# Sparse attention and a mixture-of-experts layer on one core: the gate value spread by a transfer, first weights in pieces of two blocks, v of two pairs ahead of q, a new order with more filler matmuls

## The chip, the cores and the metric

The kernel runs on one core of one Trainium2 chip. The metric is device time in microseconds (us) of the whole program, lower is better. Engines are named as in the profile: PE (matmul), PEld (weight loads of PE), DVE, ACT, POOL and SP; POOL and SP also issue DMA transfers.

## The reference

```python
# attention: q, k, v are [4 batches, 8 heads, 768 rows, 64]
block, window = (32, 16)
k_sum = k.reshape(B, H, nb, block, D).max(axis=3)
v_sum = v.reshape(B, H, nb, block, D).mean(axis=3)
scores_l = scale * np.matmul(q, k.transpose(0, 1, 3, 2))        # kept where |i - j| < 16
scores_s = scale * np.einsum('bhsd,bhnd->bhsn', q, k_sum) + np.log(block)
a = softmax(concatenate([masked scores_l, scores_s]))
attn = np.matmul(a, np.concatenate([v, v_sum], axis=2))
# mixture of experts: x is attn as [4, 768, 512]; 8 experts, F = 1024
pooled = x.mean(axis=1)
logits = pooled @ w_gate
e_idx = np.argmax(logits, axis=1)                   # one expert for each batch
gate_w = softmax(logits)[e_idx]
out[b] = gate_w[b] * (np.maximum(x[b] @ w1[e_idx[b]], 0) @ w2[e_idx[b]])
```

The expert of a batch is known only when the attention of that batch is done, so its weights (w1 and w2, 2 MB each in float32) can only be fetched then.

## The kernel before

There are four batches, and in each the 8 heads go as 4 pairs (pr 0 to 3). The work of a pair is: transpose k and q (T; in batches 1 to 3 one step for both, which takes two PSUM banks), copy them out of PSUM (own, qo), maxima over blocks of 32 (kmx, rest), scores on PE (S, two halves u), exp on ACT, mask on DVE (batches 1 to 3), weights times v on PE (O), division by the sum on DVE (norm), transpose back on PE (X), copy to xT on ACT (xo), whose running sum gives the pooled x. Vs sums v over blocks on PE, once for two pairs in batch 0 and once for four pairs in the others; DVE spreads the sums over the rows of `vblk` (Vc).

After the four pairs of a batch comes its gate: G_add, four small matmuls (G_mm, in the profile `lgps`), G_pick (largest logit and its index, which POOL loads into a register, line 718, and an exp on ACT), G_rec (reciprocal). Then POOL issues the expert's weights: w1 in four pieces at the column blocks W1CUTS, then w2 in two (G_load, lines 748 and 751; a block is 128 columns). The expert has 16 H steps (8 column blocks ft times 2 halves u; four 128x384 matmuls each, L786) with a ReLU on ACT or DVE, and 6 Y outputs (st) of two parts (four 128x512 matmuls each, L814), which ACT or DVE multiplies by the gate value and SP stores. The gate value is one number on one partition; G_bc spreads it over 128 partitions by a matmul with a row of ones (L764), and G_col copies it out of PSUM (L773).

Loads of k, q and v are issued by POOL (lines 239 and 250), strictly in POOL's order, and so are the weights. Stores are issued by SP.

The whole program is one list of 634 steps. `ORDER`, a table of numbers, sets the order in which the steps are written out, and each engine runs its steps in this order. `Plan.solve` walks through the list with the planner's costs, gives each step its engine (where ACT or DVE can do it) and PSUM bank ("one": 6 banks, "sc": one buffer for scores), and where it finds PE idle ahead of a step, sets `op.idle`, a number of filler matmuls on zeros that `warm` writes ahead of that step:

```python
op.spare = op.start - max(room, free.get(op.eng, 0.0))
...
if op.spare > 0.1 and op.start < self.warm_until:
    op.idle = int((op.spare - 0.1) / self.IDLE)
```

Nine fillers stand at the start (first_warm, L887), and 18 more among the steps of batch 0 (L878).

Of the kernel before, what the change touches and what calls it, by code (L numbers as in the profile page):

```python
# [81 lines left out]
class Plan:  # L82
# [7 lines left out]
    warm_until = 60.0  # L90
# [22 lines left out]
    def solve(self):  # L113
# [5 lines left out]
        for op in self.order:  # L119
# [21 lines left out]
            for eng, dur in op.engs:  # L141
                st = max(r, free.get(eng, 0.0))
                if eng == "pe":
                    if st < self.slow_until:
                        dur *= self.slow
                    if way != tiling:
                        dur += self.SWITCH
                if pick is None or st + dur < pick[0]:
                    pick = (st + dur, st, eng)
            op.end, op.start, op.eng = pick  # L150
            op.spare = op.start - max(room, free.get(op.eng, 0.0))
# [12 lines left out]
    def emit(self):  # L164
        for op in self.order:
            if op.fn is not None:
# [4 lines left out]
def kernel(  # L171
# [119 lines left out]
    ones_row = const.tile([1, 128], FP32, name="ones_row")  # L291
# [879 lines left out]
```

## Time and profile before

| | |
|---|---|
| median of 3 runs | 174.94 us (173.83 to 175.24) |
| the profiled execution | 176.72 us |
| its span, first to last instruction | 175.1 us |
| PE, DVE, ACT, POOL busy | 150.8, 100.2, 90.7, 43.9 us |
| mean granted PE clock | 0.932 |
| DMA packets | 60117, 26.01 MB |

The span starts with the first instruction; 1.62 us of the profiled execution lie outside it. PE is the busiest engine, but it isn't busy at full clock all the time, and which wait ends last differs from stage to stage: the stages have to be read one by one.

### The profile page before, as it was taken

Reading aid. Unit: us, or ns where it says so; the run is one execution under the profiler, and the core shown is the slowest. Engines: PE = TensorE matmul, PEld = TensorE weight load, DVE = VectorE, ACT = ScalarE, POOL = GpSimd, SP = SyncE. Lnnn points to the kernel's source line nnn. Section 1 sums busy time; section 2 is a strip of 40 time slices with the busy share of each in tenths; the row PEclk is TensorE's granted clock in tenths of the full one; section 3 lists DMA queues with packets and bytes.
Section 4 is the critical chain, followed back from the end, with each engine's and each line's share of the span. In section 5 each row is a group of like instructions: output and inputs, shape, how many; then the busy total and the mean of one; then the engine's idle time right before and its main releaser. Section 6 shows DMA issues by size and latency. Waiting matters only on the chain. (4 is left out here: it accounts for less than half of the span.)

```text
span 175.1 us, 4824 instructions
## 1 busy us (share of the span) xinstructions
PE 150.8 (86%) x2060; PEld 91.0 (52%) x2075; DVE 100.2 (57%) x247; ACT 90.7 (52%) x168; POOL 43.9 (25%) x62
## 2 busy tenths in 40 slices
PE   6697899765999969998992499899999999899990
PEld 2265566554556656464651446545566544455450
DVE  3492677957699745859985209298967402061200
ACT  2156235677566848845762067575765314244151
POOL 6994400009910000597000000270000072000000
PEclk9999569995589999999999569999999999999999
DMA  2999999997999999399999991199990059995125
GB/s 23 205 187 145 157 206 175 144 37 70 172 202 207 204 152 114 36 209 229 229 232 206 155 125 8 56 166 173 228 285 6 0 52 138 237 237 177 60 88 213
DMA packets 60117, 26.01 MB, mean 149 GB/s; under 512 B 42560, under 2 KB 57152, under 8 KB 60096
## 3 DMA queue, kind: packets, MB, share of 16 engines
q0 software_dynamic: 55968, 19.40, 126.0%
q1 hardware_dynamic: 4128, 6.31, 10.3%
q8 instruction: 16, 0.26, 0.7%
q14 instruction: 5, 0.04, 0.1%
HBM read 38.81 MB, written 6.29 MB: 258 GB/s over the span
## 5 line engine op out<-in xcount | busy, mean ns | idle before, releaser
L786 PE MATMUL hps<-xT,w_sb 128*128 128x384 bf16 x256 | 49.2, 339 | 1.1 <-DMA w_sb<-in_moe_w_dram 1.1
L814 PE MATMUL o_ps<-w_sb,hT 128*128 128x512 bf16 x171 | 42.9, 384 | 1.1 <-issue 0.5
L748 POOL DMA_DIRECT2D w_sb<-in_moe_w_dram x16 | 12.0, 765 | 96.0 <-PE tps L418 29.8
L786 PEld LDWEIGHTS <-w_sb 128*128 128x128 bf16 x256 | 24.2, 101 | 19.0 <-issue 2.7
L805 ACT ACTIVATE hT<-hps 128x384 bf16<-128x384 f32 x46 | 22.0, 491 | 21.1 <-PE hps L786 21.1
L612 ACT ACTIVATE aT<-sc 128x768 bf16<-128x768 f32 x32 | 25.9, 808 | 12.9 <-PE sc L572 6.8
L814 PEld LDWEIGHTS <-hT 128*128 128x128 bf16 x184 | 17.1, 98 | 18.1 <-issue 0.6
L828 DVE TENSOR_SCALAR o_sb<-o_ps,gcol 128x512 f32<-128x512 f32 x10 | 7.5, 750 | 21.0 <-PE o_ps L814 16.3
L649 DVE TENSOR_TENSOR xs<-ops,rv 128x384 bf16<-128x384 f32 x32 | 17.8, 558 | 1.2
L250 POOL DMA_DIRECT2D vblk<-in_v_dram x10 | 15.5, 1575 | 4.4 <-issue 3.5
L674 ACT ACTIVATE xT<-xps 128x768 bf16<-128x768 bf16 (+1 forms) x20 | 13.5, 682 | 5.1 <-PE xps L665 4.9
L803 DVE TENSOR_SCALAR hT<-hps 128x384 bf16<-128x384 f32 x18 | 9.8, 554 | 9.4 <-PE hps L786 8.9
L833 ACT ACTIVATE o_sb<-o_ps,gcol 128x512 f32<-128x512 f32 x13 | 8.9, 685 | 11.4 <-PE o_ps L814 11.2
L451 DVE TENSOR_REDUCE kmx<-kaug 128x24 bf16<-128x768 bf16 x12 | 11.3, 946 | 5.0 <-ACT kaug L428 4.9
L428 ACT COPY qT<-tps 128x768 bf16<-128x768 bf16 x12 | 9.3, 795 | 9.2 <-PE tps L418 7.9
L418 PE MATMUL tps<-identb,q_nat 96*64 96x96 bf16 x192 | 7.3, 219 | 6.5 <-DMA q_nat<-in_q_dram 4.8
L364 DVE TENSOR_TENSOR aT<-aT,seen 96x1536 bf16<-96x1536 bf16 x12 | 11.4, 948 | 1.3 <-ACT aT L612 1.3
L593 PE MATMUL sc<-qT,kaug 64*128 64x64 bf16 x288 | 8.8, 197 | 3.5 <-ACT aT L612 3.3
L531 DVE COPY vblk<-vs_sb 24x1536 bf16<-24x1536 bf16 x16 | 10.7, 671 | 1.4 <-ACT vs_sb L428 1.0
L593 PEld LDWEIGHTS <-kaug 64*128 64x128 bf16 x288 | 6.2, 98 | 9.3 <-issue 7.6
L418 PEld LDWEIGHTS <-q_nat 96*64 96x64 bf16 x192 | 5.8, 119 | 7.2 <-DMA q_nat<-in_q_dram 5.1
L508 PE MATMUL vsps<-vblk,bind 96*32 96x128 bf16 (+1 forms) x144 | 8.7, 273 | 0.8 <-DVE vblk L489 0.8
(97 smaller groups left out, 168.5 us busy)
## 6 DMA issues: line engine op xcount, KB each, us to landing
w_sb<-in_moe_w_dram POOLq DMA_DIRECT2D x12, 512.0 KB, 10.9
out_dram<-o_sb SPq DMA_DIRECT2D x23, 256.0 KB, 4.2
vblk<-in_v_dram POOLq DMA_DIRECT2D x6, 576.0 KB, 21.6
k_nat<-in_k_dram POOLq DMA_DIRECT2D x3, 768.0 KB, 15.4
q_nat<-in_q_dram POOLq DMA_DIRECT2D x3, 768.0 KB, 18.1
vblk<-in_v_dram POOLq DMA_DIRECT2D x2, 564.0 KB, 18.7
w_sb<-in_moe_w_dram POOLq DMA_DIRECT2D x8, 128.0 KB, 4.0
w_sb<-in_moe_w_dram POOLq DMA_DIRECT2D x4, 256.0 KB, 6.0
```

Of the source, the lines that this page charges most:

```text
L250: nc.gpsimd.dma_start(vb[p0:p1, n0:n1, 0:D], bass.AP(v.tensor, v.offset + ((b * H * NJ + n0) * QB - HALO + p0) * D, [[D, p1 - p0], [QB * D ...
L364: nc.vector.tensor_tensor(out=rows, in0=rows, in1=seen.unsqueeze(1).to_broadcast([R_SUM, 2 * NJ, QB]), op=ALU.mult,)
L418: nc.tensor.transpose(ps[hh * D : (hh + 1) * D, r, :], src[:, 2 * pr + hh, r * D : (r + 1) * D], identb[0:PR, 0:PR],)
L451: nc.vector.tensor_reduce(out=kmxs[b, pr].rearrange("q (j c) -> q j c", c=QB // BLK), in_=k_own(b, pr).rearrange("q j (c t) -> q j c t", t ...
L593: nc.tensor.matmul(sc[:, hh, w * QB : (w + 1) * QB], lhsT=ka[rs, pr, j, :], rhs=qT[rs, j * QB : (j + 1) * QB], start=True, stop=True, tile ...
L612: nc.scalar.activation(aT, scs.pop((b, pr, u)), ACT.Exp, scale=SCALE)
L649: nc.vector.tensor_tensor(out=xss[s][:, t0 : t0 + NW // 2], in0=ops[:, :, :, 0:D], in1=rv.unsqueeze(3).to_broadcast([128, NW // 2, 2, D]), ...
L674: nc.scalar.activation(xT[b][:, pr, us[0] * HB : (us[-1] + 1) * HB], xpss.pop((b, pr, us[0])), ACT.Copy, accum_out=red[b][:, pr, us[0] : u ...
L748: nc.gpsimd.dma_start(wts[b][0][:, :, fs], src[:, :, fs])
L786: nc.tensor.matmul(hps[:, 0:HB], lhsT=w1_sb[:, dt, ft * 128 : (ft + 1) * 128], rhs=xT[b][:, dt, u * HB : (u + 1) * HB], start=(dt == 0), s ...
L805: nc.scalar.activation(dst, hps[:, 0:HB], ACT.Relu)
L814: nc.tensor.matmul(o_ps, lhsT=hTs[b][:, ft, st * 128 : (st + 1) * 128], rhs=wts[b][1][:, ft, :], start=(ft == 0), stop=(ft == NFT - 1),)
```

## The change

The core of the difference, beside the table `ORDER` and the planner's costs (each changed by up to 0.3 us):

```diff
-    W1CUTS = [0, 1, 2, 4, 8]
+    W1CUTS = [0, 2, 4, 8]
...
     def G_bc(b):
-        def f(op):
-            gpss[b] = one_pool.tile([128, 512], FP32, name="gps", tag=op.takes[0].tag())
-            nc.tensor.matmul(
-                gpss[b][:, 0:1], lhsT=ones_row[0:1, :], rhs=gcols[b][0:1, 0:1],
-                start=True, stop=True,
-            )
-        return f
-
-    def G_col(b):
+
         def f(op):
             gcol = small.tile([128, 1], FP32, name="gcol")
-            nc.vector.tensor_copy(gcol, gpss.pop(b)[:, 0:1])
+            grec = gcols[b]
+            nc.sync.dma_start(
+                gcol, bass.AP(grec.tensor, grec.offset, [[grec.ap[0][0], 1], [0, 128], [1, 1]])
+            )
             gcols[b] = gcol
         return f
...
+    def warm(n):
+        for _ in range(n):
+            nc.tensor.matmul(idle_ps[0], lhsT=zb[:, 0:128], rhs=zb, start=True, stop=True)
...
-            op.spare = op.start - max(room, free.get(op.eng, 0.0))
+            op.spare = op.start - free.get(op.eng, 0.0)
...
-                if op.spare > 0.1 and op.start < self.warm_until:
+                if op.spare > 0.1 and not over:
...
-        {"one": 6, "sc": 1, "aT": 5, "qT": 4, "xs": 4, "hT": 2, "xT": 2, "o_sb": 4,
+        {"one": 6, "sc": 1, "aT": 5, "qT": 4, "xs": 4, "hT": 2, "xT": 2, "o_sb": 6,
...
             ve = add(("dve", 0.3), V_edge(b, g), "ve", base + g[0] - 5,
-                     [R["Lv", b, p] for p in g] + [R["count", b % 2], R["mask"]])
+                     [m, R["count", b % 2], R["mask"]])
...
-    FIRST = "k01 i0 q01 k23 i1 q23 v01 v23".split()
-    ORDER = ["kq1", "v1", "w0", "kq2", "v2", "w1", "kq3", "v3", "w2", "w3"]
+    FIRST = "k01 i0 q01 i1 k23 v01 q23 v23".split()
+    LOADS = ["e0", "kq1", "v1", "w0", "kq2", "v2", "w1", "kq3", "v3", "w2", "w3"]
```

So: the gate value goes over the partitions by a DMA that SP issues, without PE, PSUM and DVE. The first w1 piece has two column blocks, so there are three pieces. v of the first two pairs is fetched ahead of q of the last two, and V_edge follows the sum Vs. The fillers have a PSUM bank of their own, kept from the start to the first H step, they may stand ahead of any PE step up to there (`over` is true behind it), and a wait for a PSUM bank counts as idle time too. There are six output buffers in place of four. The new table has 622 steps.

Three places show how instructions move. First PE, between the gate of batch 0 (`lgps<-wg_sb,reds`) and its first H step (`hps`); `sc` are scores of batch 1, `vsps` its sum of v, `tps` its last transposes. Rows that repeat are left out. Before:

```order
L701 MATMUL lgps<-wg_sb,reds 1x8 x4
...
L418 MATMUL tps<-identb,q_nat 64x96
...
L593 MATMUL sc<-qT,kaug_90 128x64
L508 LDWEIGHTS bind
L508 MATMUL vsps<-vblk_88,bind 32x256
...
L593 MATMUL sc<-qT,kaug_90 128x64
L786 LDWEIGHTS w_sb
L786 MATMUL hps<-xT,w_sb 128x384
```

And now (`idle_ps` are fillers):

```order
L698 MATMUL lgps<-wg_sb,reds 1x8 x4
...
L871 MATMUL idle_ps<-zb 128x512
L419 LDWEIGHTS k_nat
...
L871 MATMUL idle_ps<-zb 128x512
L510 LDWEIGHTS bind
L510 MATMUL vsps<-vblk_88,bind 32x256
L871 LDWEIGHTS zb
L871 MATMUL idle_ps<-zb 128x512
...
L777 MATMUL hps<-xT,w_sb 128x384
```

Sixteen fillers stand here where there were none: 2 ahead of the last transposes, 7 ahead of the third score step, 6 ahead of the sum and 1 behind it. In all there are 45 among the steps (29 of them ahead of the gate of batch 0) in place of 18.

Second PE, around the first transposes of batch 3 (k_nat and q_nat of batch 3; `hps` and `o_ps` belong to the expert of batch 1 or, for `o_ps` before, batch 0; `ops` and `xps` to batch 2). Before:

```order
L786 MATMUL hps<-xT,w_sb 128x384
L630 LDWEIGHTS aT
L630 MATMUL ops<-vblk_87,aT 64x65
L418 LDWEIGHTS k_nat
L418 MATMUL tps<-identb,k_nat 64x96
L418 LDWEIGHTS q_nat
...
L814 MATMUL o_ps<-w_sb,hT 128x512
L786 LDWEIGHTS w_sb
L786 MATMUL hps<-xT,w_sb 128x384
```

Now:

```order
L777 MATMUL hps<-xT,w_sb 128x384
L628 LDWEIGHTS aT
L628 MATMUL ops<-vblk_87,aT 64x65
L419 LDWEIGHTS k_nat
L419 MATMUL tps<-identb,k_nat 64x96
L419 LDWEIGHTS q_nat
...
L662 MATMUL xps<-identb,xs 128x128
...
L805 MATMUL o_ps<-w_sb,hT 128x512
```

Before, 14 H steps of batch 1, 7 Y halves, 3 O and no X steps stand between the gate of batch 1 and these transposes, and two transposes of batch 2; now all 16 H steps, 10 Y halves, 4 O, 1 X and three transposes of batch 2 do.

Third POOL, the loads of v of batch 3 (`vblk_88<-in_v_dram`; the pieces of 80x64 and 96x47x64 together are pairs 2 and 3) and the load of batch 2's expert number into a register (`ix`). Before:

```order
L239 DMA q_nat<-in_q_dram 96x8x512
L250 DMA vblk_88<-in_v_dram 96x48x64
L250 DMA vblk_88<-in_v_dram 80x64
L250 DMA vblk_88<-in_v_dram 96x47x64
L718 TENSOR_LOAD ix_2207
L718 ISA x2
L748 ISA
L748 DMA w_sb<-in_moe_w_dram 128x4x128
```

Now:

```order
L241 DMA q_nat<-in_q_dram 96x8x512
L252 DMA vblk_88<-in_v_dram 96x48x64
L715 TENSOR_LOAD ix_2251
L715 ISA x2
L252 DMA vblk_88<-in_v_dram 80x64
L252 DMA vblk_88<-in_v_dram 96x47x64
L745 ISA
L745 DMA w_sb<-in_moe_w_dram 128x4x256
```

The second half of v of batch 3 now stands behind the register load, which waits for the gate of batch 2.

On SP the first two gate values (batches 0 and 1) stand ahead of the first store; the third stands behind nine stores, the fourth behind fifteen.

More of the change, by code (lines that the diff above doesn't have):

```diff
@@ L149, in solve @@
                     pick = (st + dur, st, eng)
+            over = op is self.idle_end or self.idle_end.end is not None
             op.end, op.start, op.eng = pick
-            op.spare = op.start - max(room, free.get(op.eng, 0.0))
+            op.spare = op.start - free.get(op.eng, 0.0)
             free[op.eng] = op.end
@@ L162, in solve, with emit @@
         return max(o.end for o in self.order)
-    def emit(self):
+    def emit(self, warm):
         for op in self.order:
+            warm(op.idle)
             if op.fn is not None:
@@ L303 @@
     inner = const.tile([R_SUM, 1], FP32, name="inner")
-    kline = const.tile([128, NP, S + 2 * HALO], BF16, name="kline")
+    EARLY = 1
+    klines = [
+        const.tile([128, NP, S + 2 * HALO], BF16, name=f"kline{i}") for i in range(EARLY)
+    ]
+    kmx_line = const.tile([128, EARLY, NP, NB], BF16, name="kmx_line")
     def counts(i):
@@ L326, in masks @@
     def masks(op):
-        nc.vector.memset(ones_row, 1.0)
         for hh in range(2):
@@ L395, in f @@
             bank = one_pool.tile([128, 512], FP32, name="tps", tag=op.takes[0].tag())
-            warm(op, bank)
             ps = bank[:, 0:HB].bitcast(BF16).rearrange("q (r p) -> q r p", r=RR)
@@ L449, in f @@
         def f(op):
-            kmxs[b, pr] = small.tile([128, NB], BF16, name="kmx")
+            kmxs[b, pr] = (
+                kmx_line[:, b, pr] if b < EARLY else small.tile([128, NB], BF16, name="kmx")
+            )
             nc.vector.tensor_reduce(
@@ L502, in f @@
             bank = one_pool.tile([128, 512], FP32, name="vsps", tag=op.takes[0].tag())
-            warm(op, bank)
             w = VW[b]
@@ L660, in f @@
             bank = one_pool.tile([128, 512], FP32, name="xps", tag=op.takes[0].tag())
-            warm(op, bank)
             n = NW // 2 * len(us)
@@ L783, in f @@
             hps = one_pool.tile([128, 512], FP32, name="hps", tag=op.takes[0].tag())
-            warm(op, hps)
             for dt in range(NDT):
@@ L872, in Y_store @@
         return f
-    def warm(op, tile_):
-        for _ in range(op.idle):
-            nc.tensor.matmul(
-                tile_, lhsT=zb[:, 0:128], rhs=zb[:, 0 : tile_.shape[-1]],
-                start=True, stop=True,
-            )
+    idle_ps = []
+    def warm(n):
+        for _ in range(n):
+            nc.tensor.matmul(idle_ps[0], lhsT=zb[:, 0:128], rhs=zb, start=True, stop=True)
     def first_warm(op):
-        ps = one_pool.tile([128, 512], FP32, name="wps", tag=op.takes[0].tag())
-        for _ in range(9):
-            nc.tensor.matmul(ps, lhsT=zb[:, 0:128], rhs=zb, start=True, stop=True)
+        idle_ps.append(
+            one_pool.tile([128, 512], FP32, name="idle_ps", tag=op.takes[0].tag())
+        )
+        warm(9)
     R = {}
     plan = Plan(
-        {"one": 6, "sc": 1, "aT": 5, "qT": 4, "xs": 4, "hT": 2, "xT": 2, "o_sb": 4,
+        {"one": 6, "sc": 1, "aT": 5, "qT": 4, "xs": 4, "hT": 2, "xT": 2, "o_sb": 6,
          "w": 2},
@@ L956, in attention @@
             R["Tk", b, pr], R["Tq", b, pr] = tk, tq
-            own = add(EITHER(0.86, 1.0), K_own(b, pr), "own", w, [tk] + wk)
+            own = add(EITHER(0.84, 0.98), K_own(b, pr), "own", w, [tk] + wk)
             ks.users.append(own)
-            if b == 0:
-                own.deps.append(R["count", 0])
+            if early:
+                own.deps.append(R["count", b])
                 rest = add(("dve", 1.0), K_max(b, pr), "kmx", w, [own])
             else:
-                rest = add(("dve", 1.65), K_rest(b, pr), "rest", w, [own, R["edge", b % 2]])
+                rest = add(("dve", 1.8), K_rest(b, pr), "rest", w, [own, R["edge", b % 2]])
             qt = Slot("qT")
-            qo = add(EITHER(0.86, 1.0), Q_all(b, pr), "qo", w, [tq], [qt])
+            qo = add(EITHER(0.84, 0.98), Q_all(b, pr), "qo", w, [tq], [qt])
             qs.users.append(qo)
@@ L979, in attention @@
                 R["S", b, pr, u], R["e", b, pr, u] = s, [e]
-            if b:
-                e = add(("dve", 1.05), S_mask(b, pr), "mul", w - 10, es + [R["fact"]])
+            if not early:
+                e = add(("dve", 1.08), S_mask(b, pr), "mul", w - 10, es + [R["fact"]])
                 at.users.append(e)
@@ L1019, in attention @@
                 xsl.users.append(x)
-                xo = add(("act", 0.7 if n_ == 1 else 1.02), X_out(b, pr, us), "xo", w - 5, [x],
+                xo = add(("act", 0.74 if n_ == 1 else 1.07), X_out(b, pr, us), "xo", w - 5, [x],
                          [xt] if (pr, us[0]) == (0, 0) else [])
@@ L1030, in gate @@
                 [R["x", b, p, u] for p in ALLP for u in range(2)])
-        m = add(("pe", 0.5), G_mm(b), "gate", -1000, [a], [gs])
+        m = add(("pe", 0.25), G_mm(b), "gate", -1000, [a], [gs])
         p = add(("dve", 0.6), G_pick(b), "gate", -1000, [m])
@@ L1047, in gate @@
         for c in range(2):
-            _, t = transfer(G_load(b, 1, 4 * c, 4 * c + 4), 0.8, 2.7)
+            _, t = transfer(G_load(b, 1, 4 * c, 4 * c + 4), 0.8, 2.6)
             R["w2", b, c] = t
@@ L1061, in expert @@
                 R["w", b].users.append(m)
+                if (b, ft, u) == (0, 0, 0):
+                    idle.users.append(m)
+                    plan.idle_end = m
                 o = add(EITHER(0.55, 0.6), H_out(b, ft, u), "ho", base - 165, [m],
@@ L1066, in expert @@
                 hs[ft, u] = o
-        gsl = Slot("one")
-        g = add(("pe", 0.2), G_bc(b), "gb", base + 8, [R["grec", b], hs[0, 0]], [gsl])
-        gc = add(("dve", 0.2), G_col(b), "gc", base - 165, [g])
-        gsl.users.append(gc)
+        gc = add(("sp", 2.2), G_bc(b), "gc", base - 165, [R["grec", b]])
         for st in range(NST - (b == B - 1)):
@@ L1082, in expert @@
             sl.users.append(o)
-            s = add(("sp", 0.6), Y_store(b, st), "out", 0, [o])
+            s = add(("sp", 0.45), Y_store(b, st), "out", 0, [o])
             t = add(("q", 0.75), None, "ring", 0, [s])
@@ L1111 @@
     R["fact"] = add(("dve", 0.6), factors, "const", 50, [R["ident", 1], R["mask"]])
-    for name, i, f, t in (("count", 1, counts(1), 0.8), ("edge", 1, edges(1), 1.2),
-                          ("edge", 0, edges(0), 1.2)):
-        R[name, i] = last[0] = add(("pool", t), f, "load", 0, [last[0]])
-    wsl = Slot("one")
-    fw = add(("pe", 3.6), first_warm, "warm", -2000, [], [wsl])
+    R["count", 1] = last[0] = add(("pool", 1.0), counts(1), "load", 0, [last[0]])
+    idle = Slot("one")
+    add(("pe", 3.6), first_warm, "warm", -2000, [], [idle])
     def load_now(what):
         kind, b = what[:-1], int(what[-1])
+        if kind == "e":
+            for i in (0, 1):
+                R["edge", i] = last[0] = add(("pool", 1.2), edges(i), "load", 0, [last[0]])
+            return
         if kind == "kq":
@@ L1134 @@
     after["v"](0)
-    for what in ORDER:
+    for what in LOADS:
         load_now(what)
```

37 lines of the change are left out of this document (16 added, 21 removed), and 72 rows, old and new, of the table ORDER.

## The prediction

> **What bounds the kernel now.** I read the page's parts 1 and 2 first, then cut the span along PE (PE's timeline, and windows over the stretches of slow clock), then asked for each wait which transfer ended it (POOL's timeline and the times to landing), and last the chain that ended the span.
>
> ```profile
> PE 150.8 (86%) x2060; PEld 91.0 (52%) x2075; DVE 100.2 (57%) x247; ACT 90.7 (52%) x168; POOL 43.9 (25%) x62
> PEclk9999569995589999999999569999999999999999
> ```
>
> PE is the busiest engine at 86%, but the clock line has three dips to half speed, so its busy time isn't all work. The windows give their bounds (columns: length, then busy time of PE, PEld, DVE, ACT, POOL, then PE's clock, the DMA share and GB/s):
>
> ```profile
> 14.95:18.36 3.41, 1.71 (x32) 1.27 (x32) 0.19 (x2) 2.89 (x4) 0.00 (x0) 1.00 4.49 132
> 18.36:25.16 6.80, 6.80 (x70) 4.05 (x69) 5.55 (x10) 1.25 (x3) 1.77 (x1) 0.50 2.17 183
> 35.43:38.84 3.41, 2.44 (x84) 2.09 (x83) 1.53 (x7) 2.44 (x8) 0.00 (x0) 1.00 0.73 32
> 38.84:49.08 10.24, 7.70 (x72) 4.39 (x71) 7.33 (x13) 6.16 (x10) 9.57 (x10) 0.50 0.94 120
> 96.84:103.68 6.84, 4.98 (x57) 3.31 (x59) 0.49 (x4) 1.50 (x2) 0.00 (x0) 0.50 3.64 148
> 106.00:110.00 4.00, 3.95 (x33) 2.15 (x28) 3.74 (x9) 2.62 (x7) 0.00 (x0) 1.00 0.01 1
> ```
>
> The clock was at half from 18.36 to 25.16, 38.84 to 49.08 and 96.84 to 103.68: two, three and two times 3.41 us. Ahead of the first dip PE had been busy for 1.71 of 3.41 us, ahead of the second for 2.44. Work at half clock takes double, so half of the busy time in a dip is lost: 3.40, 3.85 and 2.49 us.
>
> PE's timeline shows the gates (`lgps`, at 36.55, 69.15 and 110.30 for batches 0 to 2), the first H step and the long waits:
>
> ```profile
> 36.55 0.34 PE L701 MATMUL lgps<-wg_sb,reds 128*1 128x8 f32 x8
> 45.42 3.90 PE L786 MATMUL hps<-xT,w_sb 128*128 128x384 bf16 x12
> 62.77 0.53 PE L418 MATMUL tps<-identb,q_nat 96*64 96x96 bf16 x16 [1.50 <-DMA q_nat<-in_q_dram]
> 69.15 0.34 PE L701 MATMUL lgps<-wg_sb,red 128*1 128x8 f32 x8
> 94.61 0.53 PE L418 MATMUL tps<-identb,k_nat 96*64 96x96 bf16 x16 [2.20 <-DVE aT L364]
> 98.48 0.85 PE L418 MATMUL tps<-identb,q_nat 96*64 96x96 bf16 x16 [3.34 <-DMA q_nat<-in_q_dram]
> 110.30 0.35 PE L701 MATMUL lgps<-wg_sb,red 128*1 128x8 f32 x8
> ```
>
> What made 94.61 and 98.48 so late is seen on POOL and in the times from issue to landing:
>
> ```profile
> 12.35 0.78 POOL L239 DMA_DIRECT2D q_nat<-in_q_dram  x1
> 39.41 3.00 POOL L748 DMA_DIRECT2D w_sb<-in_moe_w_dram  x4 [19.21 <-issue]
> 45.38 3.60 POOL L250 DMA_DIRECT2D vblk<-in_v_dram  x2
> 71.80 3.00 POOL L748 DMA_DIRECT2D w_sb<-in_moe_w_dram  x4 [22.82 <-DVE kaug L469]
> 76.99 0.84 POOL L239 DMA_DIRECT2D q_nat<-in_q_dram  x1
> 80.97 1.84 POOL L250 DMA_DIRECT2D vblk<-in_v_dram  x1 [0.84 <-DMA w_sb<-in_moe_w_dram]
> 112.63 2.99 POOL L748 DMA_DIRECT2D w_sb<-in_moe_w_dram  x4 [29.82 <-PE tps L418]
> ...
> q_nat<-in_q_dram POOLq DMA_DIRECT2D x1, 768.0 KB, 17.6
> vblk<-in_v_dram POOLq DMA_DIRECT2D x1, 576.0 KB, 23.9
> w_sb<-in_moe_w_dram POOLq DMA_DIRECT2D x1, 128.0 KB, 3.3
> q_nat<-in_q_dram POOLq DMA_DIRECT2D x1, 768.0 KB, 21.4
> vblk<-in_v_dram POOLq DMA_DIRECT2D x1, 564.0 KB, 25.5
> ```
>
> The five landings are q of batch 1 (12.35 + 17.6 = 29.95), the second half of v of batch 2 (issued 1.8 into the pair at 45.38: 71.1), the first weights of batch 1 (71.80 + 3.3 = 75.1), q of batch 3 (76.99 + 21.4 = 98.4) and the last piece of v of batch 3 (106.5). So the transfers ran back to back from 39.41 to 71.1, had little to do till 75, because the gate of batch 1 came at 69.15, and then brought weights, k and q of batch 3 by 98.4, while PE stood ahead of that batch's transposes. From there PE is nearly always busy to the end:
>
> ```profile
> 170.74 0.48 ACT o_half L862
> ```
>
> PE ends at 170.74; 4.36 us of span follow, and 1.62 outside the span make 176.72. So the time is set by: the gate of batch 0, the work to the gate of batch 1, the transfers up to q of batch 3, and then PE's own work.
>
> **Part by part, along PE's gates.** Unit prices at full clock are the distances of starts:
>
> ```profile
> 57.60 0.35 PE L593 MATMUL sc<-qT,kaug 64*128 64x64 bf16 x12
> 57.88 0.38 PE L764 MATMUL gps<-grec,ones_row 1*128 1x1 f32 x2
> 58.19 0.57 PE L630 MATMUL ops<-vblk,aT 120*64 120x65 bf16 x24
> 110.57 0.53 PE L418 MATMUL tps<-identb,k_nat 96*64 96x96 bf16 x16
> 111.28 0.51 PE L418 MATMUL tps<-identb,k_nat 96*64 96x96 bf16 x16
> 140.75 7.07 PE L814 MATMUL o_ps<-w_sb,hT 128*128 128x512 bf16 x31
> 147.66 2.11 PE L786 MATMUL hps<-xT,w_sb 128*128 128x384 bf16 x12
> ```
>
> A score step is 0.28 us, the spread of the gate value (gb) 0.31, a transpose of k and q 0.71, a Y half 6.91 / 8 = 0.86.
>
> *Start to the gate of batch 0 (36.55).* The steps are the same, with 29 fillers in place of 18. In the new order the first transpose of batch 1 stands ahead of the last O and the last two X of batch 0, and it needs q of batch 1, which still lands at 29.95. From there: transpose 0.71, O and X about 0.25 each, the norm between them about 0.8, then two more transposes 1.42 and small gaps: gate at about 33.9 at best, 2.65 earlier. But PE still waits for v: q of the last two pairs now goes behind it, so v of pairs 0 and 1 lands about 2 us sooner (at some 16), and PE, through with its scores at about 14.4, stands for 1.6 us with a single score buffer. That is the kind of window that ended in the first dip. If the dip returns, its 3.40 us meet a slack of 1.1 (the fillers ahead of the wait for q): gate at about 36.2. I take **-0.3**; the other end is -2.65.
>
> *Gate of batch 0 to the first H (8.87 before).* Sixteen fillers are added. Here ACT sets the pace:
>
> ```profile
> L612 ACT ACTIVATE aT<-sc 128x768 bf16<-128x768 f32 x32 | 25.9, 808 | 12.9 <-PE sc L572 6.8
> L428 ACT COPY qT<-tps 128x768 bf16<-128x768 bf16 x12 | 9.3, 795 | 9.2 <-PE tps L418 7.9
> ```
>
> Up to the score step that stands ahead of the first H, ACT has three exps and six copies, 9 x 0.80 = 7.2 us, and the gate's exp 0.5; with the score step and two hand-overs 8.3. The fillers (16 x 0.216 = 3.5 us) lie in that shadow: PE's own steps here are 3.5 us, so 1.3 stay idle. Term **-0.6**. Without the shadow the fillers would cost up to 3.5.
>
> A rule of the Trainium skill bears on the fillers. Here the clock fell after windows in which PE was busy for 1.71 and 2.44 of 3.41 us, and stayed low for two and three windows. The Trainium skill, page "TensorE: Matmul & The Clock Gate", section "Part 1: The HAM clock gate", says that the clock halves after an idle window of about 3.4 us and returns after a busy one. The trace agrees on 3.4 us as the step of time, not on idleness: half-filled windows were enough. By the rule, no gap that I find ahead would be long enough for a dip, and the time would be that of the first rival below.
>
> *First H to the gate of batch 1 (23.73 before).* Of the second dip, 45.42 to 49.08 lies here and PE was busy in all of it: -1.83 if the fillers hold the clock. The gate moves ahead of a transpose, a Y half, a score step and gb: -(0.71 + 0.86 + 0.28 + 0.31) = -2.16. The wait of 1.50 for q of batch 2 goes: its only transpose ahead of the gate now stands at the gate, and weights come 0.76 us sooner into line (one issue less, 3.00 / 4). Term **-5.5**. Late next is that q itself: 62.7 - 0.3 - 0.76 = 61.6, against a need at about 62.
>
> *Gate of batch 1 to gate of batch 2 (41.15 before).* Two waits (2.20 and 3.34) and the dip behind them (2.49) hang on q of batch 3. The new list has two transposes, three Y halves more, a score step and gb less in this stage: +3.41, and the transposes of batch 3 stand at 27.0 us of work behind the gate in place of 21.5. The gate comes at 36.2 + 8.3 + 18.2 = 62.7, so its weights are issued (2.65 later, as 71.80 after 69.15) at 65.4, before v of batch 2 has landed at about 70: the gap in the transfers closes. First weights at 71.7, and q some 21.5 behind them, as the second block before: 93.2. PE gets there at 62.7 + 27.0 + 1.35 for small gaps = 91.1, and its k half takes 0.36: 1.7 us of wait are left, too little for a dip. Term -5.54 - 2.49 + 3.41 + 1.7 = **-2.9**.
>
> *Gate of batch 2 to the end of PE (60.44 before).* A transpose, two Y halves and two gb fewer, two score steps more: -2.49. Against it stands the second half of v of batch 3, now behind the register load on POOL. Before, the first DMA behind that load started 112.63 - 110.30 = 2.33 after the gate; the small piece and the descriptors of the large one take 0.56 and 1.8, and an empty queue needs some 4 to 5 more for 564 KB: landing 9 us behind the gate. The sum of v on PE is due at 8.2 (7.34 of work and 0.9 of gaps). Weights queue behind it, and the first H of batch 2, due at 11, wants a piece that lands at 10.3. Cost 1, between 0 and 3. Term **-1.5**.
>
> *What costs nothing.* The spread gate value: the only small transfer of SP in the profile, w_gate, landed in 1.9 us; stores took up to 7.7. Each value is issued over 8 us ahead of its use. The first stores now wait for the second gate, but six buffers hold all six outputs of batch 0. If that cover failed, once 2 to 8 us. The pieces of two blocks: -0.76 to +1 each, hidden in batches 0 to 2; in batch 3, where PE waited 0.55 for w1, the fourth block's need and landing stay close. One PSUM bank less up to the first H: 0 to 0.7, in the range. V_edge behind the sum: DVE had been waiting there.
>
> **Sum.** -0.3 - 0.6 - 5.5 - 2.9 - 1.5 = -10.8: 176.72 becomes 165.9 for a profiled execution. That one stood 1.8 above the median of the runs (174.94), so I forecast **164.0**.
>
> **The rivals.**
> 1. The clock holds from the start (the gate of batch 0 at 33.9, q of batch 3 no longer waited for): another -2.3 and -1.7, **160.0**. For it: 45 fillers, no gap over 1.6 us. Against: two dips came after half-filled windows.
> 2. The fillers don't hold the second dip, or they aren't in ACT's shadow: 1.83 comes back, and 16 fillers at half clock add up to 3.5: **168 to 169**. For it: one gap of 1.2 us, behind the last transposes of batch 1, has only a few fillers beside it, and a window of 2.44 of 3.41 didn't suffice.
> 3. The change doesn't do what it says: waits only change places, PE again stands ahead of batch 3's transposes because the transfers are the limit: stages one and two -0.9, the stage of q -2, gb -1.2, against 1 for v and a new dip 2.5, in all -0.6: **174**, within 1%, which is about what a measurement of this kernel can tell from no change.
> 4. Slower: v behind the register load. Its last piece took 25.5 us before. If it takes that again, the sum of v waits 2.3 + 25.5 - 8.2 = 19.6 us and the time is **182**; it passes the old time when the landing takes over 18 us. Against it: it took 25.5 behind weights, k and q; now nothing is in line ahead of it (at 106 to 110 the DMA moved 1 GB/s).
>
> **How the numbers follow.** Forecast 0.50, rival 1 0.18, rival 2 0.20, rival 3 0.07, rival 4 0.05. The range 158.5 to 171 holds the first three with the bounds of v (0 to 3) and of the transfers; 0.12 is left out with the last two. Faster by over 1%: 0.88, within 1%: 0.07, slower: 0.05.
>
> **What would show it.** Right: the gate of batch 1 near 63 and of batch 2 near 101; no dip between 38 and 105 longer than 3.4 us; no weights landing after a pause in the DMA line between 60 and 75; a wait of about 1 us for v ahead of the sum of v of batch 3. Wrong: a dip among the 16 fillers, `q_nat` waited for over 3 us in batch 3, or a sum of v that waits over 5.

## The result, and the profile after

The median is **162.88 us** (162.69 to 163.33, 4 runs) against 175.09 (173.83 to 175.90): a ratio of 0.931, 95% interval 0.925 to 0.937. The forecast was 164.0 with a range of 158.5 to 171. The profiled execution of the kernel after took 162.88 too, with a span of 161.2. Some executions of a kernel lie over 1.5% above its fastest: medians and ranges in this text are over all executions, ratios and their intervals rest on the faster ones alone, so a ratio need not be the quotient of two medians.

Busy time and clock, from the page:

```profile
PE 147.3 (91%) x2073; PEld 87.4 (54%) x2094; DVE 95.8 (59%) x233; ACT 95.0 (59%) x177; POOL 41.2 (26%) x58
PEclk9999999999999999999999999986999999999999
```

Of the three dips in the clock none is left in its place; there is one new dip near 108. PE's timeline at the places that the prediction spoke of (start, length, matmul, in brackets the idle time ahead of it and what ended that):

```profile
15.31 1.50 PE L510 MATMUL vsps<-vblk,bind 96*32 96x256 bf16 x12 [0.41 <-DMA vblk<-in_v_dram]
29.28 0.53 PE L419 MATMUL tps<-identb,k_nat 96*64 96x96 bf16 x16
33.20 0.34 PE L698 MATMUL lgps<-wg_sb,reds 128*1 128x8 f32 x8
42.54 1.47 PE L777 MATMUL hps<-xT,w_sb 128*128 128x384 bf16 x8
60.67 0.35 PE L698 MATMUL lgps<-wg_sb,red 128*1 128x8 f32 x8
88.47 0.51 PE L419 MATMUL tps<-identb,k_nat 96*64 96x96 bf16 x16
96.27 0.34 PE L698 MATMUL lgps<-wg_sb,red 128*1 128x8 f32 x8
107.46 1.11 PE L510 MATMUL vsps<-vblk,bind 96*32 96x128 bf16 x46 [2.64 <-DMA vblk<-in_v_dram]
110.62 1.15 PE L777 MATMUL hps<-xT,w_sb 128*128 128x384 bf16 x4
155.69 1.91 PE L834 MATMUL o_ps<-w_sb,hT 128*128 128x256 bf16 x16
```

The gates of batches 0 and 1 come at 33.20 and 60.67 (before 36.55 and 69.15), that of batch 2 at 96.27 (110.30), and PE ends at 157.60 (170.74). The transposes of batch 3 at 88.47 wait for nothing; the sum of v of batch 3 waits for 2.64 us. POOL's timeline says why, and the landings below it (the last figure is us from issue to landing):

```profile
67.78 0.82 POOL L241 DMA_DIRECT2D q_nat<-in_q_dram  x1
98.45 2.36 POOL L252 DMA_DIRECT2D vblk<-in_v_dram  x2 [27.75 <-PE o_ps L805]
100.81 2.27 POOL L745 DMA_DIRECT2D w_sb<-in_moe_w_dram  x3
```

```profile
q_nat<-in_q_dram POOLq DMA_DIRECT2D x1, 768.0 KB, 18.3
vblk<-in_v_dram POOLq DMA_DIRECT2D x1, 564.0 KB, 8.4
w_sb<-in_moe_w_dram POOLq DMA_DIRECT2D x1, 256.0 KB, 8.4
```

q of batch 3 landed at 67.78 + 18.3 = 86.1, 2.4 us ahead of its need. The last part of v stood behind the register load of batch 2's gate and landed at 107.4, 11.2 us behind that gate. The first piece of batch 2's weights, issued at 100.81, landed at 109.2.

### The profile page after: what moved, and what is told of

It reads as the page before. It is cut to its first block, busy times and chain, and to the rows that moved or that the text cites. A ratio compares the mean times of both kernels' runs of the same rounds, so it can differ in the third digit from the quotient of the medians.

```text
span 161.2 us, 4834 instructions
## 1 busy us (share of the span) xinstructions
PE 147.3 (91%) x2073; PEld 87.4 (54%) x2094; DVE 95.8 (59%) x233; ACT 95.0 (59%) x177; POOL 41.2 (26%) x58
## 4 chain that ended last, share of the span: by engine, by line
PE 74%; DMA 14%; POOL 4%; issue 2%; DVE 2%; ACT 1%; POOLq 0%
PE hps L777 27%; PE o_ps L805 22%; DMA vblk<-in_v_dram 14%; PE tps L419 5%; PE ops L628 4%; PE idle_ps L871 3%; PE sc L593 3%; PE xps L662 3%; PE vsps L510 3%; POOL vblk L252 2%; PE o_ps L834 1%; POOL k_nat L241 1%; POOL q_nat L241 1%; PE lgps L698 1%; DVE vblk L533 1%
## 5 line engine op out<-in xcount | busy, mean ns | idle before, releaser
L777 PE MATMUL hps<-xT,w_sb 128*128 128x384 bf16 x256 | 46.2, 328 | 0.0
L612 ACT ACTIVATE aT<-sc 128x768 bf16<-128x768 f32 x32 | 25.9, 811 | 12.9 <-PE sc L593 6.4
L796 ACT ACTIVATE hT<-hps 128x384 bf16<-128x384 f32 x48 | 23.0, 490 | 12.9 <-PE hps L777 12.6
L805 PEld LDWEIGHTS <-hT 128*128 128x128 bf16 x184 | 16.9, 98 | 18.3 <-issue 0.6
L745 POOL DMA_DIRECT2D w_sb<-in_moe_w_dram x12 | 9.0, 758 | 63.4 <-issue 26.6
L824 ACT ACTIVATE o_sb<-o_ps,gcol 128x512 f32<-128x512 f32 x19 | 13.0, 686 | 10.7 <-PE o_ps L805 5.8
L871 PE MATMUL idle_ps<-zb 128*128 128x512 bf16 x46 | 14.7, 430 | 2.5 <-DVE zb L272 1.3
L794 DVE TENSOR_SCALAR hT<-hps 128x384 bf16<-128x384 f32 x16 | 8.7, 551 | 8.7 <-PE hps L777 8.7
L642 DVE RECIPROCAL rv<-ops 128x6 f32<-128x6 f32 x32 | 6.0, 188 | 8.1 <-PE ops L628 8.0
L533 DVE COPY vblk<-vs_sb 24x1536 bf16<-24x1536 bf16 x16 | 9.0, 580 | 1.9 <-ACT vs_sb L429 1.5
L510 PE MATMUL vsps<-vblk,bind 96*32 96x128 bf16 (+1 forms) x144 | 6.7, 248 | 3.3 <-DMA vblk<-in_v_dram 3.3
L628 PE MATMUL ops<-vblk,aT 120*64 120x65 bf16 x384 | 9.1, 197 | 0.5 <-ACT qT L429 0.3
L628 PEld LDWEIGHTS <-aT 120*64 120x64 bf16 x384 | 7.4, 111 | 3.3 <-issue 2.1
## 6 DMA issues: line engine op xcount, KB each, us to landing
w_sb<-in_moe_w_dram POOLq DMA_DIRECT2D x12, 512.0 KB, 11.2
k_nat<-in_k_dram POOLq DMA_DIRECT2D x3, 768.0 KB, 15.2
q_nat<-in_q_dram POOLq DMA_DIRECT2D x3, 768.0 KB, 18.3
```

Of the source, the lines that this page charges most:

```text
L510: nc.tensor.matmul(vs_ps[BLK * c : BLK * (c + 1), :, :], lhsT=bind[:, j, :], rhs=vb[0:R_SUM, 2 * w * c : 2 * w * (c + 1), j, 0:D], start=( ...
L612: nc.scalar.activation(aT, scs.pop((b, pr, u)), ACT.Exp, scale=SCALE)
L628: nc.tensor.matmul(ops[w * QB : (w + 1) * QB, t, hh, :], lhsT=weights(b, pr, hh, j), rhs=vb[0:NR, 2 * pr + hh, j, 0 : D + 1], start=True, ...
L777: nc.tensor.matmul(hps[:, 0:HB], lhsT=w1_sb[:, dt, ft * 128 : (ft + 1) * 128], rhs=xT[b][:, dt, u * HB : (u + 1) * HB], start=(dt == 0), s ...
L796: nc.scalar.activation(dst, hps[:, 0:HB], ACT.Relu)
L805: nc.tensor.matmul(o_ps, lhsT=hTs[b][:, ft, st * 128 : (st + 1) * 128], rhs=wts[b][1][:, ft, :], start=(ft == 0), stop=(ft == NFT - 1),)
```

## The experiments

In the comparisons with the kernel after, times are medians and stand against its 162.88; ratios are to the kernel before in the same session, whose median was 175.1 to 176.9.

**1. No fillers between steps.**

```diff
 def emit(self, warm):
     for op in self.order:
-        warm(op.idle)
+        warm(0)
```

> The kernel after, with every step as it is, but with none of the 45 filler matmuls that stand between steps (the nine at the very start stay). Theory (the fillers hold the clock): PE is then idle for about 4 of the 9.3 us behind the gate of batch 0 and for about 3 us in the stretch from 9 to 18, and both early dips come back: 3.4 us at half clock near 15 to 25, of which the fillers' own places ahead of the wait for q of batch 1 absorb 1.3, and 7 to 10 us at half clock from about 40 on; 162.9 + 2 to 6 = 165 to 169. Rival (the new order alone removed the waits, and with them the dips): no dip, 162 to 163, because what the fillers filled was idle anyway.

Measured: 165.68 (165.20 to 167.03), ratio 0.949 (0.943 to 0.955), 2.8 us more. The clock line of the page has the first two dips back:

```profile
PEclk9955579998589999999999999995999999999998
```

So the fillers do hold the clock there, and they are worth 2.8 of the 12.2 us between the two kernels. The other 9.4 are there without them.

**2. The 16 late fillers alone left out.** From the gate of batch 0 on, `warm(0)`.

> The kernel after without the 16 fillers between the gate of batch 0 and the first H alone; the 29 ahead of them stay. Theory (these 16 hold the second dip): PE is busy for about 4.1 of the 9.3 us from 33.2 to 42.5, the clock falls at about 37 to 41 and stays at half for two or three windows, so half of the busy time in 7 to 10 us is lost: 165 to 167, and nothing changes ahead of 33. Rival one (16 fillers cost PE time that they don't bring back, since ACT's shadow is not that long): 161.5 to 162.5. Rival two (no matter either way): 162.9 within 0.8.

Measured: 163.87 (163.60 to 164.06), ratio 0.936 (0.932 to 0.940): 1.0 us more, where 2 to 4 were expected. A window over the dip (length, then PE, PEld, DVE, ACT and POOL busy, PE's clock), and PE's timeline:

```profile
35.23:45.47 10.24, 9.02 (x113) 5.64 (x113) 8.54 (x16) 6.99 (x12) 8.82 (x9) 0.50 1.33 140
```

```profile
35.33 0.85 PE L421 MATMUL tps<-identb,k_nat 96*64 96x96 bf16 x16 [1.57 <-ACT qT L431]
42.11 2.74 PE L779 MATMUL hps<-xT,w_sb 128*128 128x384 bf16 x8
```

The dip is back, 35.23 to 45.47, and half of 9.02 us of work is lost in it. Yet the first H comes at 42.11, 0.43 *sooner* than with fillers. A good part of the loss up to there lies in ACT's shadow, but not all: from the gate to the first H it is 8.97 us here, 8.05 with seven fillers and no dip (experiment 3), and 9.34 with the sixteen, which cost time themselves. Behind the first H the dip costs 3.36 / 2 = 1.7; less 0.43 that is about 1.2. So the 1.0 measured is the dip's price less that of the fillers. My expectation had priced the whole dip, and the fillers at nothing.

**3. Half of the late fillers.** Seven of the 16: from the gate of batch 0 on, `warm(op.idle // 2)`.

> The kernel after with half of the fillers behind the gate of batch 0 (7 of the 16 stay, in the same places), so that PE is busy for about 60% of the time from 33.2 to 42.5 instead of 81%. Theory (before, windows of 3.41 us in which PE was busy for 50 and 71% of the time ended in a dip; so 60% doesn't hold the clock): the dip comes back between 36 and 46, and the time is that without the 16, 163.9 (163.5 to 164.3). Rival (only a gap of some 2 us or more in one piece brings a dip): no dip, and 162.0 to 162.9, since fewer fillers hold up what follows.

Measured: 162.23 (162.06 to 162.99), ratio 0.934 (0.917 to 0.951): 0.65 below the kernel after, with times that overlap. Where a gap ended in a dip in experiment 2, the clock stays (PE's and PEld's timelines, then windows: from the gate to the first H, one of 3.42 us around the gap, and the dip that this execution has near 108):

```profile
33.64 0.10 PEld L873 LDWEIGHTS <-zb 128*128 128x128 bf16 x1
35.28 0.53 PE L421 MATMUL tps<-identb,k_nat 96*64 96x96 bf16 x16 [1.57 <-ACT qT L431]
41.14 1.47 PE L779 MATMUL hps<-xT,w_sb 128*128 128x384 bf16 x8
```

```profile
33.09:41.14 8.05, 5.29 (x121) 3.75 (x120) 6.40 (x19) 6.19 (x11) 5.53 (x7) 1.00 2.32 117
33.36:36.78 3.42, 1.85 (x61) 1.60 (x60) 2.99 (x10) 2.62 (x6) 1.17 (x2) 1.00 3.70 105
108.46:111.87 3.41, 3.41 (x22) 1.53 (x21) 2.23 (x4) 1.97 (x4) 0.00 (x0) 0.50 1.14 285
```

The 1.57 is more than the true gap: one of the seven fillers stands in it, whose weight load is on record (33.64) and whose matmul is not. At the same place the trace of experiment 12, which has that record, shows 1.25. PE was busy for 5.29 of 8.05 us by the records, 66%, or 71% with the two fillers (0.216 us each) that lack one, at full clock, and the first H came 1.40 sooner than in the kernel after. So my reading that a 60% share brings a dip fell in this execution; experiment 12 shows that the clock isn't sure to hold either.

**4. q of pairs 2 and 3 first again.**

```diff
-    FIRST = "k01 i0 q01 i1 k23 v01 q23 v23".split()
+    FIRST = "k01 i0 q01 i1 k23 q23 v01 v23".split()
```

> The kernel after with the two first loads in the old order, q of pairs 2 and 3 ahead of v of pairs 0 and 1; steps and fillers are as in the kernel after. Theory (v came in time because it went first): v lands about 2 us later, at 17.3, PE waits some 2.4 us ahead of the first sum of v with nothing to fill it, and either 0.8 us are lost (2.1 less the 1.3 us of fillers ahead of the wait for q of batch 1) or, if the first dip comes back, another 1 to 1.7: 163.7 to 165.5. Rival (the wait for q of batch 1 at 29.4 sets the gate whatever comes earlier): 162.9 within 0.5.

Measured: 164.73 (163.51, 163.63, 165.82 and 169.63), ratio 0.941 (0.932 to 0.950). The fillers are held at those of the kernel after. In the profiled execution (163.51), PE's timeline has

```profile
17.31 1.50 PE L510 MATMUL vsps<-vblk,bind 96*32 96x256 bf16 x12 [0.68 <-DMA vblk<-in_v_dram]
34.86 0.34 PE L698 MATMUL lgps<-wg_sb,reds 128*1 128x8 f32 x8
```

The sum of v is 2.0 later and the gate 1.66, without a dip up to there: nearly all of the delay goes through to the gate. The fillers ahead of the wait for q of batch 1 give nothing back (I had counted 1.3), because they are written into PE's list and run even when q has landed. At the end 0.6 of it is left in this execution; the times scatter too much to say more of what the load order is worth.

**5. The gate of batch 1 later in the kernel after.** ORDER around it, shortened (320 is the gate's matmul, 321 the pick, 323 and 325 the first pieces; 256, 283 and 274 are transposes of batch 2); the steps that ACT and DVE share are held on their engines:

```diff
-    ..., 319, 320, 224, 266, 321, 323, ..., 325, ..., 256, 283, ..., 274, 255, ...
+    ..., 319, 224, 266, ..., 256, 283, ..., 274, 320, 321, 323, 325, 255, ...
```

> The kernel after with the gate of batch 1 (its matmul, the pick, and the issue of the first two pieces of weights) moved behind three transposes of batch 2, two Y halves and a score step: 0.87 x 2 + 0.71 x 3 + 0.28 = 4.2 us later, at about 64.9; nothing else moves. Theory (the early gate keeps the transfers in line, so that q of batch 3 lands ahead of its transposes): the first weights land at 73.3 instead of 69.1, 1.2 us behind the due time of the first H of batch 1 (72.1), q of batch 3 at 90.3 instead of 86.1, 1.8 us behind the due time of the first transpose (88.5): 162.9 + 1.8 = 164.7, 164 to 166.5 with a dip behind the wait. Rival (the place of the gate only shifts work between stages): 162.9 within 0.5.

Measured: 167.07 (166.98 to 167.28), ratio 0.954 (0.949 to 0.960), 4.2 more. PE's timeline:

```profile
66.07 0.34 PE L696 MATMUL lgps<-wg_sb,red 128*1 128x8 f32 x8
72.72 0.82 PE L775 MATMUL hps<-xT,w_sb 128*128 128x384 bf16 x4 [0.41 <-DMA w_sb<-in_moe_w_dram]
75.78 2.12 PE L775 MATMUL hps<-xT,w_sb 128*128 128x384 bf16 x12 [1.96 <-DMA w_sb<-in_moe_w_dram]
92.62 0.53 PE L417 MATMUL tps<-identb,q_nat 96*64 96x96 bf16 x16 [0.98 <-DMA q_nat<-in_q_dram]
```

The gate is 5.4 us later, and waits for weights (0.41 and 1.96) and for q of batch 3 (0.98) come back, 3.35 us that the kernel after doesn't have. The place of the gate is no mere shift of work. The largest of the waits, for the second piece of weights, I had not foreseen.

**6. The gate of batch 1 earlier in the kernel before**, ahead of two transposes of batch 2 (259, 268) and their score step (263), again with the shared steps held on their engines:

```diff
-    ..., 256, 259, 166, ..., 268, 170, 322, 236, 263, 269, 264, 323, 271, 324, 270, ..., 326, ...
+    ..., 256, 166, ..., 170, 322, 236, 323, 324, 326, 259, 260, 262, 261, 268, 263, 269, 264, 271, 270, ...
```

> The kernel before with one move: the gate of batch 1 (its matmul, the pick, the issue of the first piece of weights) ahead of the first two transposes of batch 2 and their score step, which stood in front of it; fillers, pieces and gate value as before. Theory (a gate that comes earlier brings the weights, and behind them k and q of batch 3, earlier into the DMA line): gate at about 66.0 instead of 69.15 (1.50 of wait for q of batch 2, 2 x 0.71 and 0.28), the wait of 1.50 goes, q of batch 3 lands at about 95.2 instead of 98.4, and the wait of 3.34 shrinks to about 1.6: 175.1 - 3.2 = 172, down to 169.5 if the third dip goes with it. Rival (the place of the gate only shifts work between stages): 175 within 1. Second rival (the transposes of batch 2 come late, and the score steps and ACT behind them): over 176.

Measured: 172.12 (169.58 to 175.83), 6 runs, ratio 0.990 (0.959 to 1.020): the times scatter and don't settle it by themselves. The trace (of the run of 169.58) does show the mechanism, in PE's timeline and the page's clock line:

```profile
34.76 0.35 PE L699 MATMUL lgps<-wg_sb,reds 128*1 128x8 f32 x8
63.80 0.35 PE L699 MATMUL lgps<-wg_sb,red 128*1 128x8 f32 x8
93.98 0.53 PE L416 MATMUL tps<-identb,q_nat 96*64 96x96 bf16 x16 [2.03 <-DMA q_nat<-in_q_dram]
```

```profile
PEclk9879999965699999789999999999999999999999
```

From gate to gate it is 29.04 us (63.80 less 34.76) instead of 32.60, q of batch 3 lands at 94.0 instead of 98.4, one wait of 2.03 is left of 2.20 and 3.34, and the dip behind it is gone (a shorter one stands near 70). One move in the old order brings what the prediction's third and fourth terms rest on: an earlier gate, and with it an earlier q of batch 3.

**7. The gate value by transfer alone, in the kernel before.** `G_bc` is that of the kernel after, `G_col` does nothing.

> The kernel before with one part of the change: the gate value is spread by SP's transfer where the matmul and the copy from PSUM stood, order and fillers as before. Theory (each matmul step is worth its place on PE, 0.31 us, in four batches, and the transfer's landing is hidden): 175.1 - 0.6 to 1.2 = 173.9 to 174.5, since only the steps behind the last dip count in full. Rival (the transfer is late for the first output of a batch, 2.7 to 7 us of landing in the kernel after): over 176.

Measured: 175.12 (12 runs), ratio 0.998 (0.994 to 1.002): between -1.0 and +0.3 us. The four matmuls' 1.2 us on PE don't come back in full, and no loss through a late value is seen.

**8. The first piece as two transfers again**, in the kernel after.

```diff
-                nc.gpsimd.dma_start(wts[b][0][:, :, fs], src[:, :, fs])
+                cuts = [0, 1, 2] if c0 == 0 else [c0, c1]
+                for a, z in zip(cuts, cuts[1:]):
+                    fs = slice(a * 128, z * 128)
+                    nc.gpsimd.dma_start(wts[b][0][:, :, fs], src[:, :, fs])
```

> The kernel after with the first weights of each gate again in two transfers of one column block each (steps, order and fillers as in the kernel after): POOL issues one DMA more per batch, 0.75 us, and the first H can start on a quarter of w1's half. Theory (the pieces are hidden in all batches): 162.9 within 0.8. Rival one (the larger first piece is late for the first H of batch 2, where it took 8.4 us to land and PE started its H 1.4 us behind it): the smaller piece gains up to 0.5 there. Rival two (the extra issue delays what stands behind it in batch 1, and with it q of batch 3): 163.6.

Measured: 164.19 (163.04 to 164.77, 6 runs), ratio 0.935 (0.931 to 0.940). Its interval overlaps that of the kernel after (0.925 to 0.937), so the pieces are worth between nothing and about 1.5 us. Most of the difference goes with the clock: the two executions at a mean clock of 0.989 took 163.04 and 163.21 (the kernel after at 0.989: 162.88 and 162.89), the four at 0.976 to 0.979 took 164.16 to 164.77. The profiled one (164.77) has a dip of two steps of 3.41 us near 108, where the kernel after has one:

```profile
107.67:114.50 6.83, 6.36 (x82) 3.42 (x82) 2.73 (x6) 2.66 (x5) 0.00 (x0) 0.50 1.22 246
```

Whether the split pieces make that dip longer stays open.

**9. The second half of v of batch 3 ahead of the register load.** One step, 402, goes right behind the first half's (400):

```diff
-    ..., 364, 400, 353, ..., 469, 232, 402, 405, 471, ...
+    ..., 364, 400, 402, 353, ..., 469, 232, 405, 471, ...
```

> The kernel after with one step moved: the load of the second half of v of batch 3 is issued right behind that of its first half (near 70) and no longer behind the register load for the weights of batch 2 (98.5). Theory (that place cost the wait of 2.65 us ahead of the sum of v and the dip that follows, 1.5): the load lands behind the first half, 94.9 + 8.4 = 103.3, 1.5 us ahead of the sum of v at 104.8; wait and dip are gone, weights of batch 2 are issued 2.4 us sooner: 162.9 - 4.1 = 158.7, 158 to 160. Rival (the transfers are the limit there, and the wait only moves: v lands at 107 all the same, or PE waits as long ahead of the first H of batch 2): 161.5 to 163.5.

Measured: **158.79** (157.90 to 159.64), ratio 0.908 (0.902 to 0.914): 4.1 us better than the kernel after. From the page, POOL's timeline and PE's:

```profile
PE 147.0 (94%) x2073; PEld 87.5 (56%) x2094; DVE 94.8 (60%) x233; ACT 94.9 (61%) x177; POOL 41.4 (26%) x58
```

```profile
69.56 4.46 POOL L250 DMA_DIRECT2D vblk<-in_v_dram  x3 [0.87 <-DVE grec L752]
98.70 2.26 POOL L743 DMA_DIRECT2D w_sb<-in_moe_w_dram  x3 [24.68 <-PE o_ps L803]
```

```profile
104.69 0.85 PE L508 MATMUL vsps<-vblk,bind 96*32 96x128 bf16 x48
106.63 0.81 PE L775 MATMUL hps<-xT,w_sb 128*128 128x384 bf16 x4
```

The sum of v no longer waits, the weights of batch 2 are issued 2.1 sooner, and the first H of batch 2 comes at 106.63 instead of 110.62: 4.0 us, the whole gain.

**10. Fillers in that wait.** Twelve fillers ahead of the sum of v of batch 3, in the kernel after:

```diff
             vs_ps = bank[:, 0 : 2 * w * D].rearrange("p (h d) -> p h d", d=D)
+            if b == 3:
+                for _ in range(12):
+                    nc.tensor.matmul(bank, lhsT=zb[:, 0:128], rhs=zb, start=True, stop=True)
```

> The kernel after with 12 fillers (12 x 0.216 = 2.6 us) written ahead of the sum of v of batch 3, into the bank that this step has already: the wait for v from 104.8 to 107.4 stays, but PE isn't idle in it. Theory (the wait of 2.65 us brought the dip at 107.9, and the dip cost 1.2 to 1.5): no dip, 161.4 to 161.7. Rival (the dip's work lies beside a wait for the weights of batch 2 that land at 109.2, so it costs next to nothing): 162.5 to 163. Second rival (the dip has another cause than the gap): it stays, and the time is that of the kernel after.

Measured: 162.83 (162.72 to 163.14), ratio 0.930 (0.926 to 0.934), the same as the kernel after. PE's timeline and the clock line:

```profile
104.49 2.75 PE L510 MATMUL vsps<-zb 128*128 128x512 bf16 x12
109.56 0.81 PE L780 MATMUL hps<-xT,w_sb 128*128 128x384 bf16 x4
111.47 1.47 PE L780 MATMUL hps<-xT,w_sb 128*128 128x384 bf16 x8 [0.81 <-DMA w_sb<-in_moe_w_dram]
```

```profile
PEclk9999999999999999999999999999999999999999
```

In all six executions the mean clock was 0.996 to 1.000, against 0.985 to 0.998 in the kernel after, so the dip goes with the gap. The gap isn't sure to bring one: in experiment 2 the same wait was there, and the clock stayed at full speed behind it (PE's timeline and a window of that run):

```profile
108.44 0.85 PE L512 MATMUL vsps<-vblk,bind 96*32 96x128 bf16 x46 [2.52 <-DMA vblk<-in_v_dram]
110.32:113.73 3.41, 3.41 (x63) 2.02 (x61) 3.17 (x5) 2.90 (x6) 0.00 (x0) 1.00 1.14 281
```

And the dip of one step cost nothing: without it the first H comes 1.06 sooner, and the next ones wait for weights. Behind the register load stand v *and* the weights; the dip lay beside the weights' landing. So the 1.3 us that experiment 9 brought beyond the wait didn't come from the clock alone: the weights had to come sooner too (sooner weights alone weren't tried).

**11 and 12. Combinations.** The step of experiment 9 without any filler between steps, and with half of the late ones.

> The step of v_ahead, and none of the 45 fillers between steps. Theory (the fillers' worth of 2.8 us, measured in the kernel after, lies ahead of batch 1's gate and has nothing to do with v of batch 3): 158.8 + 2.8 = 161.6, 161 to 163. Rival (without the wait for v PE's early delay is absorbed elsewhere, as the dip at 107.9 was): 159 to 160.

> The step of v_ahead (the second half of v of batch 3 loaded behind its first half) and that of half_late_fillers (7 of the 16 late fillers) together. Theory (they act at different places, and what the fewer fillers gain ahead of the first H stays): 158.8 - 0.65 = 158.1, 157.6 to 158.8. Rival (the first H comes sooner but waits for its weights, or a dip comes back in some executions): 158.8 to 160.

Measured: 161.61 without fillers (160.56 to 162.42), ratio 0.923 (0.917 to 0.929), and 158.17 with half (157.51 to 161.08), ratio **0.904** (0.900 to 0.908). The fillers' 2.8 us are there again, so they and v act apart. The version with half of them is the fastest median here, but no faster than experiment 9 within the scatter; its profiled run is the one of 161.08, and it has the dip that experiment 3 did not have (the clock line, PE's timeline, windows ahead of the dip and over it):

```profile
PEclk9999999996569999999999999999999999999999
```

```profile
35.42 0.53 PE L419 MATMUL tps<-identb,k_nat 96*64 96x96 bf16 x16 [1.25 <-ACT qT L429]
43.60 2.74 PE L777 MATMUL hps<-xT,w_sb 128*128 128x384 bf16 x8
```

```profile
33.33:36.74 3.41, 2.16 (x67) 1.64 (x66) 3.00 (x10) 2.44 (x6) 0.99 (x2) 1.00 3.90 112
36.74:46.98 10.24, 9.46 (x75) 4.32 (x74) 6.15 (x13) 5.41 (x10) 8.11 (x8) 0.50 1.08 153
```

The other six executions took 157.51 to 158.97. So the one with this dip is some 3 us longer, not 1.0 as in experiment 2; a single execution doesn't show that the dip is all of it.

Not tried alone were the six output buffers, the later V_edge, the fillers' own PSUM bank and the rest of the new order. How much of the 9.4 us each of them brings isn't shown.

## Why the prediction was right, point by point

The sign and the range held, and so did the mechanism of the third and fourth terms. Two terms of the sum were too careful, by 3.1 and 2.7 us, and two too kind, by 1.1 and 2.4; that these errors cancel in part is luck. Of the signs named, the clock between 38 and 105 and the unbroken transfers came as said, the gates came still sooner (60.67 and 96.27 for 63 and 101), and the wait for v, 2.64 us, lies between the 1 of the right and the 5 of the wrong. Stages run along PE's gates.

| Stage | Term | Measured in the profiled executions |
|---|---|---|
| start to gate of batch 0 | -0.3 (best end -2.65) | -3.35 |
| to the first H | -0.6 | +0.47 |
| to the gate of batch 1 | -5.5 | -5.60 |
| to the gate of batch 2 | -2.9 | -5.55 |
| to the end of PE | -1.5 | +0.89 |
| sum | -10.8 | -13.14 |

- *Start.* I let the first dip return after a gap of 1.6 us ahead of the sum of v. The gap was 0.41: v landed at 15.2 instead of some 16, and fillers stood ahead of the score steps. That is rival 1 (chance 0.18), and not the forecast, up to the gate of batch 2; it gave 160.0, and what kept the time from there is the last stage.
- *To the first H.* This step was half right: ACT's shadow takes some of the fillers, but 16 are more than fit. With seven the first H comes 1.40 sooner (experiment 3); with none, and a dip, 0.43.
- *To the gate of batch 1.* Right within 0.1; the gates' order, the wait for q of batch 2 and the part of the dip behind the first H behaved as worked out.
- *To the gate of batch 2.* The cause was right, by experiments 5 and 6. The size was not: I put q 21.5 us behind the first weights and so 30.5 behind the gate; it landed 25.4 behind the gate (86.1 less 60.67) and 17.0 behind the first weights, which landed at 69.1 (issued at 63.31, 5.8 to land). Why that stretch was shorter isn't shown. So of the 1.7 of left-over wait there was none, and small gaps shrank too.
- *To the end.* This step failed. The landing of v behind the register load was put at the gate plus 9 and came at plus 11.2; the large piece alone took 8.4 us where I gave it 1.8 for its descriptors and 4 to 5 more, a figure for which I had no row. The weights behind it were put 10.3 behind the gate and came 12.9 behind it (109.2), so that the first H of batch 2 started 14.35 behind it, not 11. The cost that I put at 1 was 4.1 us (experiment 9). Rival 4 had the mechanism, at a wait of 19.6.
- *The clock.* The Trainium skill, page "TensorE: Matmul & The Clock Gate", section "Part 1: The HAM clock gate", says that the clock halves after an idle window of about 3.4 us. The dips here needed less: gaps of 1.57 (experiment 2) and 2.64 us (the kernel after) stood ahead of one, while 2.52 us in experiment 2 brought none. The same section says that the window is free-running and doesn't reset with the kernel. The trace agrees: the same stage's dip starts at 35.23 in experiment 2 and at 36.74 in experiment 12, 1.5 us apart, with the gates 0.1 apart. But that doesn't explain experiment 3 against 12. Counted back in steps of 3.413 us from its dip at 108.46, experiment 3 has a step at 36.78, nearly where the dip of experiment 12 starts; PE was busy for 1.85 us (some 2.1 with the filler that lacks a record) and for 2.16 us in the step ahead, and only the second ended in a dip. What decides stays open.
- *The offset.* Between the profiled executions the sum missed 3.0 us (165.9 against 162.88): 2.3 in the stages and 0.7 behind PE's end. That the median was missed by only 1.1 is due to the 1.8 that I took off because the profiled execution of before stood above its median; that of after stands at its own.

## What to carry to other kernels

Look at everything that an in-order queue holds behind a wait, not only the piece whose landing the profile names: moving one load ahead of a register load was worth 4.1 us here, as much as a gate 5.4 us earlier. Price a clock dip by what waits for PE behind it, and a filler by its own time: a dip of 10 us partly in ACT's shadow cost 1.0 more than the sixteen fillers that hold it, and one of 3.4 us beside a transfer cost nothing. Fillers are work that runs whether or not the wait is there; half as many gave the same time or a little less, but not the same clock in every execution.

## What was not expected of the hardware

- The clock depends on more than the program. With no late fillers (experiment 2) the mean granted clock was 0.966 to 0.968 in four of four executions, with seven it lay between 0.968 and 1.000 over the seven of experiment 12, and with all 16 (experiment 9) between 0.995 and 1.000.
- The gate value's transfer, half a KB, took 2.7 to 7.0 us to land in the kernel after, against 1.9 for the small load at the start. None of PE's waits goes back to it. The fourth, issued behind fifteen stores at 141.95, landed at 148.95, and the first output of batch 3 was multiplied from 150.71 on. The rows are the shortest and the longest of the four landings:

```profile
gcol<-grec SPq DMA_DIRECT2D x1, 0.5 KB, 2.7
gcol<-grec SPq DMA_DIRECT2D x1, 0.5 KB, 7.0
```
